# The weights' output rows parked in DRAM, lower halves of the weight sums on POOL, and a new issue list in an attention and FFN kernel

## The chip, the cores and the metric

One core of a Trainium2 chip. The metric is the device time of one execution in microseconds; for the kernel before it is 601.78 us, the median of 3 runs (601.61 to 604.16).

## The reference

```python
# q, k, v: (4, 8, 768, 64) fp32; blocks of 32 rows, a window of 16
k_sum = k.reshape(B, H, 24, 32, D).max(axis=3)
v_sum = v.reshape(B, H, 24, 32, D).mean(axis=3)
scores_l = where(|i - j| < 16, q @ k.T / 8, -1e9)      # local keys
scores_s = q @ k_sum.T / 8 + log(32)                    # 24 block maxima
a = softmax(concat[scores_l, scores_s])
x = (a @ concat[v, v_sum]) -> (3072 tokens, 512)
h = x @ w_in                        # 512 -> 2048
out = (s * relu(h)**2 + b) @ w_out  # 2048 -> 512
```

## The kernel before

The 3072 tokens are worked in 12 chunks c of 256 tokens, three to a batch entry. A chunk goes through attention by head pairs p (0 to 3), then through the FFN by 16 blocks f of 128 of the 2048 hidden columns; q is a pair of such blocks (0 to 7). Each fp32 matrix product is three TensorE products of upper and lower fp32r halves.

Every instruction is issued by `do(name)` from a list written out by hand, FIRST_ORDER and then REST_ORDER, under a manual schedule: the list's order is the order of every engine's and queue's instructions. Engines are in order, so an instruction that waits holds all behind it on its engine. The DMAs of this kernel all go through SP's queue (q1). Names in the list: a letter or two for the function, then numbers, chunk first.

- Attention of chunk c: u loads queries and keys (L253), k fills in the block maxima on POOL (L266), x and t load and fill the values (L260, L271), S scores on PE (L309), M masks on DVE (L332), E exponentials on ACT (L351), np and tb normalize and transpose on DVE (L365 to L368, L390), V values on PE (L441), X and y the upper and lower halves of the result (L227 on ACT, L457 on DVE). L loads the raw keys of a batch entry and K takes their block maxima (L154, L159); lv, vs, vm, sv do the same for the values' block means (L168, L175, L181, L186).
- FFN: H.f hidden block (L509, 24 matmuls to two blocks). For chunks 0 to 3, J, G, a, b square, scale and split it and P.f projects it (L554) into two "po" accumulators; O empties one of them on ACT (a copy at L227), z stores the rows (L701). For chunks 4 to 11, re, sq, af, sr, us, ls are the same steps (L567, L571, L575, L580 to L584, L591, L595), and p.q.n (L674) projects a pair of blocks by seven products of 128x256 blocks, n = 0 to 6, instead of eight. Its accumulators are called m, x, y, z: m lies in the "pav" bank, x and y in the two "po" banks, z in "pt". Three of the seven right-hand sides are sums of blocks of w_out, which are streamed from DRAM into a ring (j, L614), a fourth one is kept in the weights' own place (kc, L618).
- Weights: w, i, o load a block's w_in and w_out columns (L117), A and Bi, Bo, D turn them to fp32 tiles `w_f` (ACT L125 and L126, DVE L134 and L135), h makes the upper halves (L227), l the lower ones (DVE L147). `w_f` and `w_l` tiles share one pool of 16 buffers (wring). Once l has run, the fp32 tile is given up.
- Weight sums, while chunks 2 and 3 run: for each q, sw has six POOL steps, in which the first two (L629, 128x512) add upper and lower halves of the w_out part to get fp32 again and four more (L631 to L637, 128x256) make the sums. uw rounds to the upper half on ACT (L640, 128x1024), lw takes the lower half on DVE (L644, 128x1024), zw stores the two (L648, 512 KB each) to the DRAM tile `combos`. They work in `spare`, of three pieces of 1024 columns that are used in turn; `spare` and the ring of the later chunks are one buffer after the other in the same place, so the first j waits for the last zw.

The values' accumulator of head pairs 0 and 1 of chunk c is chosen in `values`: "po" where `c > SEVEN` (SEVEN is 4), else "pav", but for a few early chunks.

Of the kernel before, what the change touches and what calls it, by code (L numbers as in the profile page):

```python
# [14 lines left out]
ALU = mybir.AluOpType  # L15
# [21 lines left out]
UNIT = T + NSUB * KR + 2  # L37

# [6 lines left out]
def windowed_attention_then_relu2_ffn(ctx, tc, qk, vwin, kt, vt, kq, vrow, wp, out):  # L45
# [7 lines left out]
    ctx.enter_context(tc.tile_pool(name="gap_arena", bufs=1)).tile([P, 16], F32, name="gap_arena")  # L53
# [4 lines left out]
    ctx.enter_context(tc.tile_pool(name="gap_acts", bufs=1)).tile([P, 48], F32, name="gap_acts")  # L58
# [9 lines left out]
    spare = arena.tile([P, 3072], F32, name="spare", tag="ring")  # L68
    combos = kept.tile([NF // 2, P, 4, 2, 256], F32, name="combos")

# [65 lines left out]

    def upper_weights(f, other=False):
        j = f
        if j % 2 == 0:
            held["wh", j // 2] = slot(F32R, "wh")  # L140
        w_h[f] = held["wh", j // 2][:, 1024 * (j % 2) : 1024 * (j % 2 + 1)]
        copy(other, w_h[f], w_f[f])

    def lower_weights(f):

        w_l[f] = wring.tile([P, 1024], F32R, name="wl", tag="ring")
        nc.vector.tensor_tensor(w_l[f], w_f.pop(f), w_h[f].bitcast(F32), ALU.subtract)  # L147
# [271 lines left out]
    def values(c, p):  # L419
# [3 lines left out]
        elif c < 2 or p % 2 == 0:  # L423
            if c == 2:
                o_of[c, p] = ps_s.tile([P, 2 * T], F32, name="pav", tag="ps")
            elif c > SEVEN and p == 0:
                o_of[c, p] = ps_po.tile([P, 2 * T], F32, name="pav", tag="po")
            elif together(c) and p:
                o_of[c, p] = ps_t.tile([P, 2 * T], F32, name="pav", tag="pt")
            else:  # L430
                o_of[c, p] = ps_v.tile([P, 2 * T], F32, name="pav")
# [165 lines left out]
    def ring_part(c, q, n):  # L597
        if "ring" not in held:
            held["ring"] = arena.tile([P, 3072], F32R, name="ring", tag="ring")
# [8 lines left out]
        k = 512 * (3 * (q % 2) + n)  # L608
# [14 lines left out]

    def sums_of_weights(q, n):
        t = piece(2 * q)
        b11, b12, b21, b22 = (t[:, 256 * k : 256 * (k + 1)] for k in range(4))
        if n < 2:
            w = [x[2 * q + n][:, 512:].bitcast(F32) for x in (w_h, w_l)]
            nc.gpsimd.tensor_tensor(t[:, 512 * n : 512 * (n + 1)], *w, ALU.add)  # L629
        elif n == 2:  # L630
            nc.gpsimd.tensor_tensor(b22, b22, b12, ALU.add)  # L631
        elif n == 3:
            nc.gpsimd.tensor_tensor(b12, b12, b11, ALU.subtract)
        elif n == 4:
# [4 lines left out]
    def upper_weight_sums(q):  # L639
        nc.scalar.copy(piece(2 * q + 1).bitcast(F32R), piece(2 * q))  # L640

    def lower_weight_sums(q):
        t = piece(2 * q)
        nc.vector.tensor_tensor(t.bitcast(F32R), t, piece(2 * q + 1), ALU.subtract)  # L644

    def store_weight_sums(q, n):
        src = piece(2 * q + 1 - n)
# [55 lines left out]
    def evict(c, t, other=False):  # L703
# [4 lines left out]
    FIRST_ORDER = (  # L708
# [23 lines left out]
    )  # L732
    REST_ORDER = (
# [247 lines left out]
```

## Time and profile before

| | |
|---|---|
| median of 3 runs | 601.78 us (601.61 to 604.16) |
| the profiled execution | 602.11 us |
| its span | 600.4 us |
| busy: PE, DVE, ACT, POOL | 583.3, 438.6, 349.4, 298.8 us |
| DMA | 127.34 MB, mean 212 GB/s |
| mean granted TensorE clock | 0.994 |

The span is what the profiler saw between the first and the last instruction; the execution is 1.71 us longer. PE is busy 97% of the span. Times in the rows are counted from the span's start. In brackets stands the idle time of the engine ahead of an instruction and what released it.

### The profile page before, as it was taken

To read this page: it belongs to the slowest core of one execution; us is meant where nothing else is said; L and a number is where in the kernel's file an instruction comes from. 1 tells how busy PE (TensorE), PEld (TensorE's weight loads), DVE (VectorE), ACT (ScalarE), POOL (GpSimd) and SP (SyncE) were. 2 spreads that over 40 slices of the span, in tenths; PEclk is the share of its full clock that TensorE was granted. 3 is DMA by queue.
4 is the path that set the end of the run, shared out by engine and by line. 5 is a ranking of instruction groups with operands and counts; after the bars stand their busy time and mean duration, and the time that the engine had idled before them with its cause. 6 is when DMAs were issued, how large, how long until landed. Compare 5 with 4: busy or idle time off the path is not lost.

```text
span 600.4 us, 15345 instructions
## 1 busy us (share of the span) xinstructions
PE 583.3 (97%) x5816; PEld 554.0 (92%) x5816; DVE 438.6 (73%) x1033; ACT 349.4 (58%) x808; POOL 298.8 (50%) x499
## 2 busy tenths in 40 slices
PE   7999999999999999899999999999999999999996
PEld 6798898889799898799999999999999999999996
DVE  6999988799689699686688689588588488322323
ACT  5999999275496673733563564563563563433432
POOL 4330012591594563355655755745745745635643
PEclk9999999999999999799999999999999999999999
DMA  8999633064634974876776886766766766575540
GB/s 336 398 409 374 232 127 115 1 212 125 208 124 139 337 243 147 273 262 219 257 257 182 276 249 190 265 187 193 250 177 203 246 176 187 164 236 145 184 145 35
DMA packets 65401, 127.34 MB, mean 212 GB/s; under 512 B 7408, under 2 KB 17648, under 8 KB 65328
## 3 DMA queue, kind: packets, MB, share of 16 engines
q1 hardware_dynamic: 65328, 126.38, 63.4%
q8 instruction: 45, 0.74, 0.5%
q14 instruction: 28, 0.23, 0.1%
HBM read 111.52 MB, written 14.68 MB: 210 GB/s over the span
## 4 chain that ended last, share of the span: by engine, by line
PE 58%; DVE 16%; ACT 12%; DMA 8%; issue 3%; SPq 2%; POOL 1%; DVEq 0%; ACTq 0%; POOLq 0%
PE ph L509 28%; PE acc L674 24%; DVE pT L390 6%; PE pav L441 2%; DMA wraw<-in_wp_dram 2%; ACT wraw L125 2%; ACT wraw L126 2%; DMA ring<-combos 2%; DVE gs L541 2%; PE po L554 2%; ACT spare L351 2%; DVE spare L644 2%; PE ps L309 1%; DMA vraw<-in_vt_dram 1%; DMA combos<-spare 1%
## 5 line engine op out<-in xcount | busy, mean ns | idle before, releaser
L595 DVE TENSOR_TENSOR gs<-g,gs 128x896 fp32r<-128x896 f32 x64 | 71.1, 1112 | 97.6 <-ACT gs L591 97.1
L575 POOL TENSOR_SCALAR g<-g,sb_col 128x512 f32<-128x512 f32 x64 | 68.0, 1062 | 131.0 <-ACT g L571 118.2
L567 ACT ACTIVATE g<-ph 128x512 f32<-128x512 f32 x64 | 38.3, 598 | 158.5 <-PE ph L509 144.8
L390 DVE STREAM_TRANSPOSE pT<-qk 32x256 f32<-32x256 f32 x288 | 125.5, 436 | 4.8
L674 PE MATMUL acc<-wh,gs 128*128 128x256 f32 x512 | 121.2, 280 | 0.4 <-DVE gs L595 0.4
L509 PE MATMUL ph<-xh,wl 128*128 128x256 f32 x760 | 118.7, 278 | 0.2 <-DVE wl L147 0.2
L509 PE MATMUL ph<-xh,wh 128*128 128x256 f32 x760 | 117.3, 276 | 0.0
L509 PE MATMUL ph<-xl,wh 128*128 128x256 f32 x760 | 117.3, 276 | 0.0
L509 PEld LDWEIGHTS ph<-xh,wl 128*128 128x128 f32 x760 | 103.0, 188 | 4.1 <-DVE wl L147 1.0
L509 PEld LDWEIGHTS ph<-xl,wh 128*128 128x128 f32 x760 | 100.7, 188 | 0.0
L509 PEld LDWEIGHTS ph<-xh,wh 128*128 128x128 f32 x760 | 100.4, 188 | 0.0
L674 PE MATMUL acc<-ring,gs 128*128 128x256 f32 x558 | 96.4, 281 | 1.9 <-DMA ring<-combos 1.9
L674 PEld LDWEIGHTS acc<-wh,gs 128*128 128x128 f32 x512 | 91.3, 188 | 1.6 <-issue 0.9
L674 PEld LDWEIGHTS acc<-ring,gs 128*128 128x128 f32 x558 | 78.8, 188 | 2.6 <-DMA ring<-combos 2.5
L554 PE MATMUL po<-wh,gs 128*128 128x512 f32 x224 | 76.7, 394 | 0.1
L674 PE MATMUL acc<-wl,gs 128*128 128x256 f32 x256 | 71.3, 278 | 0.0
L591 ACT CAST gs<-g 128x896 fp32r<-128x896 f32 x64 | 59.9, 937 | 17.9 <-PE acc L674 7.1
L271 POOL COPY vw<-vsum 24x256 f32<-24x256 f32 x88 | 40.0, 490 | 45.2 <-DMA vw<-in_vwin_dram 18.1
L351 ACT ACTIVATE qk<-qk,mn 128x120 f32<-128x120 f32 x144 | 55.0, 384 | 6.5 <-DVE mn L332 5.7
L554 PE MATMUL po<-wl,gs 128*128 128x512 f32 x128 | 50.2, 392 | 0.0
L554 PEld LDWEIGHTS po<-wh,gs 128*128 128x128 f32 x224 | 42.1, 188 | 8.6 <-DVE gs L541 0.3
L580 POOL TENSOR_TENSOR g<-g 128x256 f32<-128x256 f32 x64 | 47.3, 738 | 4.7
(134 smaller groups left out, 919.2 us busy)
## 6 DMA issues: line engine op xcount, KB each, us to landing
ring<-combos SPq DMA_DIRECT2D x186, 256.0 KB
wraw<-in_wp_dram SPq DMA_DIRECT2D x32, 512.0 KB
qk<-in_qk_dram SPq DMA_DIRECT2D x44, 369.0 KB
vw<-in_vwin_dram SPq DMA_DIRECT2D x48, 256.0 KB
combos<-spare SPq DMA_DIRECT2D x16, 512.0 KB
out_dram<-o SPq DMA_DIRECT2D x24, 256.0 KB
kraw<-in_kt_dram SPq DMA_DIRECT2D x12, 384.0 KB
vraw<-in_vt_dram SPq DMA_DIRECT2D x12, 252.0 KB
```

What stands on the lines that cost most here:

```text
L125: nc.scalar.activation(top, top, AF.Prelu, scale=2.0**-112, alpha=2.0**32)
L271: nc.gpsimd.tensor_copy(vw_t[c, p][WIN:KR, e], vsum[bi][WIN : WIN + NB, 2 * p + e, :].unsqueeze(1).to_broadcast([NB, NSUB, D]),)
L351: nc.scalar.activation(pr, pr, AF.Exp, bias=mn_of[c, p][:, n : n + 1], scale=-1.0, accum_out=sums_of(c, p)[:, n : n + 1])
L390: nc.vector.transpose(to[BLOCK * k : BLOCK * (k + 1), :, rows], src)
L509: nc.tensor.matmul(ph, w[:, kc * P : (kc + 1) * P], x[:, kc], start=(n == 0), stop=(n == len(terms) - 1))
L554: nc.tensor.matmul(po[c, t], a[:, t * P : (t + 1) * P], w[:, 512:], start=(f == 0 and n == 0), stop=(f == NF - 1 and n == len(terms) - 1),)
L567: nc.scalar.activation(gg[c, q][:, : 2 * T], ph_of.pop((c, q)), AF.Relu)
L575: nc.gpsimd.tensor_scalar(g, g, s_col, b_col, ALU.mult, ALU.add)
L580: nc.gpsimd.tensor_tensor(g[:, 4:6], g[:, 0:1].to_broadcast([P, 2, P]), g[:, 1:3], ALU.subtract)
L591: nc.scalar.copy(halves[c, q][0], gg[c, q][:, P:])
L595: nc.vector.tensor_tensor(gl, gg.pop((c, q))[:, P:], gh.bitcast(F32), ALU.subtract)
L674: nc.tensor.matmul(to, g[:, k], w, start=(q == 0 and side == 0 and m == 0), stop=(q == NF // 2 - 1 and m == 2 and side == (bank != "m")),)
```

## The change

1. `park_weights` (pk0 to pk15) stores the fp32 tile's w_out part (128x512, 256 KB) to a DRAM tile `parked` after its conversion, and `w_f` is not given up by `lower_weights` any more. `load_parked` (lp0 to lp7) brings the parts of two blocks back (512 KB) into a piece of `spare`. The two POOL adds that had made fp32 out of the halves are gone, so sw has four steps.
2. The lower halves of the sums are two POOL subtracts of 128x512 (lw q.0 and q.1) instead of one DVE subtract of 128x1024.
3. The sums are worked in piece 0 or 1 by turns, and their upper halves always lie in piece 2.
4. Two unused gap tiles of 16 and 48 columns go; the arena is 3136 columns, of which the ring's parts begin at 16, so the ring's address stays.
5. In `values`, chunk 5's first accumulator is "pav" instead of "po".
6. One new list, ORDER. PE's instructions keep their order; SP, ACT, DVE and POOL get another one from chunk 2 on, and on SP the parks stand from u3.1 on.

The diff without the list:

```diff
+RING = 3136
...
-    ctx.enter_context(tc.tile_pool(name="gap_arena", bufs=1)).tile([P, 16], F32, name="gap_arena")
...
-    ctx.enter_context(tc.tile_pool(name="gap_acts", bufs=1)).tile([P, 48], F32, name="gap_acts")
...
-    spare = arena.tile([P, 3072], F32, name="spare", tag="ring")
+    spare = arena.tile([P, RING], F32, name="spare", tag="ring")[:, :3072]
     combos = kept.tile([NF // 2, P, 4, 2, 256], F32, name="combos")
+    parked = kept.tile([NF, P, 512], F32, name="parked")
...
+    def park_weights(f):
+        nc.sync.dma_start(parked[f], w_f[f][:, 512:])
...
-        nc.vector.tensor_tensor(w_l[f], w_f.pop(f), w_h[f].bitcast(F32), ALU.subtract)
+        nc.vector.tensor_tensor(w_l[f], w_f[f], w_h[f].bitcast(F32), ALU.subtract)
...
-            elif c > SEVEN and p == 0:
+            elif c > SEVEN + 1 and p == 0:
...
-            held["ring"] = arena.tile([P, 3072], F32R, name="ring", tag="ring")
+            held["ring"] = arena.tile([P, RING], F32R, name="ring", tag="ring")
...
-        k = 512 * (3 * (q % 2) + n)
+        k = 16 + 512 * (3 * (q % 2) + n)
...
+    def load_parked(q):
+        t = piece(q % 2).rearrange("p (f d) -> p f d", f=2)
+        nc.sync.dma_start(t, parked[2 * q : 2 * q + 2].rearrange("f p d -> p f d"))
+
     def sums_of_weights(q, n):
-        t = piece(2 * q)
-        b11, b12, b21, b22 = (t[:, 256 * k : 256 * (k + 1)] for k in range(4))
-        if n < 2:
-            w = [x[2 * q + n][:, 512:].bitcast(F32) for x in (w_h, w_l)]
-            nc.gpsimd.tensor_tensor(t[:, 512 * n : 512 * (n + 1)], *w, ALU.add)
+        b11, b12, b21, b22 = (piece(q % 2)[:, 256 * k : 256 * (k + 1)] for k in range(4))
+        if n == 0:
...
     def upper_weight_sums(q):
-        nc.scalar.copy(piece(2 * q + 1).bitcast(F32R), piece(2 * q))
-
-    def lower_weight_sums(q):
-        t = piece(2 * q)
-        nc.vector.tensor_tensor(t.bitcast(F32R), t, piece(2 * q + 1), ALU.subtract)
+        nc.scalar.copy(piece(2).bitcast(F32R), piece(q % 2))
+
+    def lower_weight_sums(q, n):
+        t, hi = (piece(k)[:, 512 * n : 512 * (n + 1)] for k in (q % 2, 2))
+        nc.gpsimd.tensor_tensor(t.bitcast(F32R), t, hi, ALU.subtract)
...
-        src = piece(2 * q + 1 - n)
+        src = piece((2, q % 2)[n])
...
-    FIRST_ORDER = (
...
-    REST_ORDER = (
+    ORDER = (
...
-        for name in (FIRST_ORDER + " " + REST_ORDER).split():
+        for name in ORDER.split():
```

SP's queue from the last unit of chunk 3 on, before (`wraw` are weight tiles, `kraw` raw keys, `qk` units, `out_dram` the first rows of the result):

```order
L253 DMA qk<-in_qk_dram 128x738
L154 DMA kraw<-in_kt_dram 128x768
L117 DMA wraw<-in_wp_dram 128x1024 x4
L253 DMA qk<-in_qk_dram 128x738 x2
L117 DMA wraw<-in_wp_dram 128x1024 x6
L154 DMA kraw<-in_kt_dram 128x768
L260 DMA vw<-in_vwin_dram 128x512
L701 DMA out_dram<-o 128x512 x2
```

and after (`parked` are the new stores; line numbers are 3 higher):

```order
L256 DMA qk<-in_qk_dram 128x738
L138 DMA parked<-wf 128x512 x9
L157 DMA kraw<-in_kt_dram 128x768
L117 DMA wraw<-in_wp_dram 128x1024 x4
L256 DMA qk<-in_qk_dram 128x738 x2
L138 DMA parked<-wf 128x512
L117 DMA wraw<-in_wp_dram 128x1024 x2
L138 DMA parked<-wf 128x512 x2
L117 DMA wraw<-in_wp_dram 128x1024 x2
L138 DMA parked<-wf 128x512 x2
L117 DMA wraw<-in_wp_dram 128x1024 x2
L157 DMA kraw<-in_kt_dram 128x768
```

Nine stores now stand ahead of the raw keys and of the weight tiles that follow, and five more between the later weight tiles.

ACT at the start of chunk 4's FFN, before (L567 and L571 are re and sq, L591 us, L640 the cast of the weight sums, L181 a mean of values, L227 with `o<-po` O3.0):

```order
L571 ACTIVATE g<-g 128x512
L640 CAST spare<-spare 128x1024
L567 ACTIVATE g<-ph 128x512
L591 CAST gs<-g 128x896
L571 ACTIVATE g<-g 128x512
L181 ACTIVATE vmean<-vhalf 96x64
L567 ACTIVATE g<-ph 128x512
L591 CAST gs<-g 128x896
L227 COPY o<-po 128x512
L571 ACTIVATE g<-g 128x512
L567 ACTIVATE g<-ph 128x512
L227 CAST xh<-pav 128x512
```

and after:

```order
L570 ACTIVATE g<-ph 128x512
L574 ACTIVATE g<-g 128x512
L570 ACTIVATE g<-ph 128x512
L574 ACTIVATE g<-g 128x512
L594 CAST gs<-g 128x896
L230 COPY o<-po 128x512 x2
L570 ACTIVATE g<-ph 128x512
L594 CAST gs<-g 128x896
L574 ACTIVATE g<-g 128x512
L570 ACTIVATE g<-ph 128x512
L230 CAST xh<-pav 128x512
```

The cast and the mean have left this place, and the two copies out of "po" stand right behind the first us.

SP's queue ahead of the ring's first loads, before (L648 are the stores of the weight sums, L253 units of chunk 6, L186 and L168 the values' block means, L614 the ring):

```order
L648 DMA combos<-spare 512x1x256
L253 DMA qk<-in_qk_dram 128x738
L648 DMA combos<-spare 512x1x256
L253 DMA qk<-in_qk_dram 128x738 x3
L186 DMA vsum<-vmean 24x64 x4
L168 DMA vraw<-in_vt_dram 96x672
L701 DMA out_dram<-o 128x512
L614 DMA ring<-combos 128x512 x6
```

and after:

```order
L651 DMA combos<-spare 512x1x256
L621 DMA wh<-combos 128x256
L256 DMA qk<-in_qk_dram 128x738 x2
L621 DMA wh<-combos 128x256
L621 DMA wl<-combos 128x256
L651 DMA combos<-spare 512x1x256
L621 DMA wh<-combos 128x256
L621 DMA wl<-combos 128x256
L617 DMA ring<-combos 128x512 x6
L256 DMA qk<-in_qk_dram 128x738 x2
```

The ring's loads now stand two kept sums behind the last store, and ahead of the last two units and of the means.

## Rows read from the trace of the kernel before

**Rows 1.** The page's first line.
```profile
span 600.4 us, 15345 instructions
```

**Rows 2.** PE's waits: engine, line, what it waited for: us in total, times, longest.
```profile
PE pav L441 <- issue: 2.9, 1, 2.9
PE acc L674 <- DMA ring<-combos: 1.9, 2, 1.2
PE ps L309 <- POOL qk L266: 1.0, 2, 0.6
```

**Rows 3.** Timeline of PE, 238 to 262: start us, us, engine line op out<-in xcount [idle before].
```profile
238.48 0.62 PE L509 MATMUL ph<-xh,wh 128*128 128x256 f32 x4
242.01 3.68 PE L441 MATMUL pav<-pT,vw 120*64 120x64 f32 x64 [2.91 <-issue]
...
260.00 0.62 PE L674 MATMUL acc<-ring,gs 128*128 128x256 f32 x3 [1.23 <-DMA ring<-combos]
...
261.88 0.62 PE L509 MATMUL ph<-xh,wl 128*128 128x256 f32 x4
```

**Rows 4.** Windows: stretch, us; busy of PE, PEld, DVE, ACT, POOL; PEclk, DMA, GB/s.
```profile
243.00:246.00 3.00, 3.00 (x59) 2.88 (x60) 0.69 (x1) 1.63 (x4) 2.81 (x8) 0.50 0.66 174
```

**Rows 5.** The chain of waits, one chunk later: start us, us, engine, out, line, count.
```profile
293.35 2.02 PE pav L441 x64
...
297.17 5.15 PE acc L674 x42
...
307.49 2.73 PE ph L509 x24
```

**Rows 6.** Timeline of ACT, 240 to 242.
```profile
240.00 0.60 ACT L567 ACTIVATE g<-ph 128x512 f32<-128x512 f32 x1 [6.98 <-DVE gs L595]
...
241.32 0.59 ACT L227 COPY o<-po 128x512 f32<-128x512 f32 x1
```

**Rows 7.** Timeline of DVE, 232 to 240.
```profile
232.13 5.87 DVE L390 STREAM_TRANSPOSE pT<-qk 32x256 f32<-32x256 f32 x13
...
238.83 1.08 DVE L595 TENSOR_TENSOR gs<-g,gs 128x896 fp32r<-128x896 f32 x1
```

**Rows 8.** Timeline of PE, 158 to 164.
```profile
158.19 2.08 PE L441 MATMUL pav<-pT,vw 120*64 120x64 f32 x64
...
163.46 0.50 PE L554 MATMUL po<-wh,gs 128*128 128x512 f32 x1
```

**Rows 9.** Groups by line and shape: count, busy us, mean ns, idle before.
```profile
L629 POOL TENSOR_TENSOR spare<-wh,wl 128x512 f32<-128x512 f32 x16 | 23.4, 1478 | 3.2 <-DMA combos<-spare 1.6 <-DVE spare L644 1.4
L644 DVE TENSOR_TENSOR spare<-spare 128x1024 fp32r<-128x1024 f32 x8 | 10.6, 1327 | 2.8 <-ACT spare L640 2.7
L175 DVE TENSOR_REDUCE vhalf<-vraw 96x21 f32<-96x672 f32 x12 | 10.0, 843 | 0.4 <-DMA vraw<-in_vt_dram 0.4
```

**Rows 10.** Windows at loads, at stores, and at both.
```profile
54.00:57.00 3.00, 3.00 (x25) 2.84 (x24) 2.83 (x5) 3.00 (x6) 0.00 (x0) 1.00 1.02 414
57.00:60.00 3.00, 3.00 (x15) 2.38 (x13) 2.48 (x4) 3.00 (x6) 0.00 (x0) 1.00 0.56 213
126.00:129.00 3.00, 3.00 (x24) 2.84 (x23) 2.96 (x19) 2.54 (x12) 2.88 (x5) 1.00 0.98 299
186.50:187.00 0.50, 0.50 (x6) 0.50 (x6) 0.49 (x2) 0.50 (x2) 0.42 (x2) 1.00 0.96 373
187.00:187.50 0.50, 0.50 (x7) 0.50 (x6) 0.49 (x2) 0.50 (x1) 0.50 (x1) 1.00 0.39 148
```

**Rows 11.** Timelines of SP, ACT, DVE and PE, 64 to 83.
```profile
64.04 0.33 SPq L154 DMA_DIRECT2D kraw<-in_kt_dram  x1
...
73.50 1.14 ACT L125 ACTIVATE wraw<-wraw 128x1024 f32<-128x1024 f32 x1 [0.89 <-DMA wraw<-in_wp_dram]
...
81.34 1.21 DVE L147 TENSOR_TENSOR wl<-wf,wh 128x1024 fp32r<-128x1024 f32 x1
...
82.70 0.71 PE L509 MATMUL ph<-xh,wl 128*128 128x256 f32 x4
```

More of the change, by code (lines that the diff above doesn't have):

```diff
@@ L622, in piece @@
         return spare[:, 1024 * n : 1024 * (n + 1)]
+    def load_parked(q):
+        t = piece(q % 2).rearrange("p (f d) -> p f d", f=2)
+        nc.sync.dma_start(t, parked[2 * q : 2 * q + 2].rearrange("f p d -> p f d"))
     def sums_of_weights(q, n):
-        t = piece(2 * q)
-        b11, b12, b21, b22 = (t[:, 256 * k : 256 * (k + 1)] for k in range(4))
-        if n < 2:
-            w = [x[2 * q + n][:, 512:].bitcast(F32) for x in (w_h, w_l)]
-            nc.gpsimd.tensor_tensor(t[:, 512 * n : 512 * (n + 1)], *w, ALU.add)
+        b11, b12, b21, b22 = (piece(q % 2)[:, 256 * k : 256 * (k + 1)] for k in range(4))
+        if n == 0:
+            nc.gpsimd.tensor_tensor(b22, b22, b12, ALU.add)
+        elif n == 1:
+            nc.gpsimd.tensor_tensor(b12, b12, b11, ALU.subtract)
         elif n == 2:
[L631 to L634, printed above, removed]
             nc.gpsimd.tensor_tensor(b11, b11, b22, ALU.subtract)
@@ L705, in evict @@
         copy(other, out_of[c, t], po[c, t])
-    FIRST_ORDER = (
[23 rows of a table removed]
-    )
-    REST_ORDER = (
[159 rows of a table removed]
+    ORDER = (
[181 rows of a table added]
     )
@@ L907, in windowed_attention_then_relu2_ffn @@
         "Y": hidden_part, "H": hidden, "J": activate, "G": scaled, "a": upper_rows, "b": lower_rows,
-        "P": project, "O": evict, "z": store_rows, "h": upper_weights, "l": lower_weights,
-        "af": affine, "cr": clear_rim, "cb": combine, "kc": keep_combo, "j": load_combo, "lv": load_v,
-        "ls": lower_sums, "lw": lower_weight_sums, "np": normalize_pair, "p": project_seven, "re": rectified,
-        "sv": spread_v, "sq": squares, "zw": store_weight_sums, "sr": sums_of_rows, "sw": sums_of_weights,
-        "tb": turned_blocks, "us": upper_sums, "uw": upper_weight_sums, "vm": v_mean, "vs": v_sum,
+        "P": project, "O": evict, "z": store_rows, "h": upper_weights, "l": lower_weights, "pk": park_weights,
+        "af": affine, "cr": clear_rim, "cb": combine, "kc": keep_combo, "j": load_combo, "lp": load_parked,
+        "lv": load_v, "ls": lower_sums, "lw": lower_weight_sums, "np": normalize_pair, "p": project_seven,
+        "re": rectified, "sv": spread_v, "sq": squares, "zw": store_weight_sums, "sr": sums_of_rows,
+        "sw": sums_of_weights, "tb": turned_blocks, "us": upper_sums, "uw": upper_weight_sums, "vm": v_mean,
+        "vs": v_sum,
     }
```

363 rows, old and new, of tables (FIRST_ORDER, ORDER, REST_ORDER) are left out of this document.

## The prediction

> **What bounds the kernel now.** The page comes first: the span is 600.4 us [rows 1], and its list of busy times puts TensorE (PE) at 97% of it. So only what lets PE stand idle, runs it at the lower clock, or takes matmuls away can move the time. The diff takes none away, and PE's instructions stand in the same order, so I read PE's waits [rows 2]. Those that come after the first weights are few: 2.9 us at the values of an attention chunk (L441), 1.9 us at the streamed ring (L674), 1.0 us at scores (L309). The timeline of PE places the first two in one stretch [rows 3]. The last matmul of H4.7 starts at 238.48 and takes 0.62; V5 starts only at 242.01, after 2.91 us of nothing. What follows is slower too: V5 takes 3.68 us [rows 3], where the same step of the next chunk takes 2.02 in the chain of waits [rows 5]. The granted clock says why: it is 0.50, the 1.2 GHz level, between 243 and 246 [rows 4], right behind the idle stretch. Then come two waits for the ring, the one with its row 1.23 us long [rows 3].
>
> So the stretch is measured whole. Unstalled, V5 could start when H4.7's last matmul lets go; 24 such matmuls take 2.73 us [rows 5], so the last four are through in 0.45 and V5 is due at 238.93. H4.10 starts at 261.88 [rows 3]: 22.95 us later. The same list of products one chunk later runs from 293.35 to 307.49 [rows 5]: 14.14 us. The excess is **8.81 us**, of which only 2.91 is the idle time itself.
>
> The second place is one chunk earlier: V3 starts at 158.19 and P2.8 at 163.46 [rows 8], 5.27 us, against 293.35 to 297.17 = 3.82 [rows 5] for the same V and S work. The excess is **1.45 us**.
>
> **Why V5 waits.** Before, the accumulator of V5.0 is one of the two "po" banks, so it needs O3.0 to have emptied it. O3.0 is ACT's copy at 241.32, 0.59 long [rows 6], and ends 0.1 before V5. ACT is in order: ahead of it stands re4.2 (L567, 240.00), which sat 6.98 us for ls4.0 on DVE (L595). ls4.0 runs at 238.83, behind 5.87 us of transposes of chunk 5 and a block sum of 0.88 [rows 7]. So DVE's backlog reaches PE by way of ACT's order.
>
> **The change part by part.**
>
> *Order and accumulator.* O3.0 and O3.1 move ahead of re4.2 on ACT, and V5.0 goes to the "pav" bank, which chunk 4's values left long ago. Either alone cuts the chain. What is late next: V5 itself needs chunk 5's transposes, which ended at 232.13 + 5.87 = 238.00 even before [rows 7], 0.9 us ahead of 238.93; p4.0.0 needs ls4.0 and, newly, y5.0 out of "pav". In the new order ls4.0 and ls4.1 stand directly behind the transposes. X5.0 on ACT stands behind re4.3; with H4.7's last matmul ending at 239.1, re4.3 (0.60 [rows 6]) ends at 239.7; X5.0, a copy of the size of O3.0's 0.59, at 240.3; y5.0, narrower than ls4.0's 1.08 [rows 7], by 241.4. p4.0.0 is due at 238.93 + 3.82 = 242.75. Slack 1.3 us.
>
> *DVE's load ahead of V5.* Three lower halves (lw5 to lw7) of 1327 ns and three block sums of 843 ns [rows 9] leave DVE there: 3 × 1.33 + 3 × 0.84 = 6.5 us. K2.0 and K2.1, which each wait for a transfer, come before chunk 5's normalization instead. So the transposes end about 231.5, or at worst where they do now.
>
> *The ring.* Its first six loads were issued behind the last store of sums and other transfers; now that store is issued at about P3.11 and the loads at H4.2, ahead of the second pair of chunk 6's units and of z3.0. The two waits go. These edits take the whole of it: **−8.81**, taken whole since each rung of the chain is cut and the next reader has slack. Bounds: nothing goes (0), or all.
>
> *S4.* P2.8's stall is two waits for POOL's fills [rows 8], which wait for chunk 4's units, whose buffers are freed by chunk 3's transposes. Those transposes now stand grouped ahead of the block sums, and the loads of u4.0 to u4.3 stand earlier: **−1.45**, between −1.45 and 0.
>
> *POOL.* Sixteen adds of 128x512 at 1478 ns go [rows 9], sixteen subtracts of the same shape come: no change there. DVE loses eight operations of 1327 ns, 10.6 us [rows 9], hidden under PE except as told above. ACT's eight casts stay. Cost 0; if POOL were late, uw would stand in ACT's queue with the a and G of chunks 2 and 3 behind it (a rival below).
>
> *Parking.* Sixteen stores of 256 KB and eight loads of 512 KB join SP's queue. The loads (4.2 MB in 110 us) lie where no wait of PE names a transfer. The stores matter early: nine of them (2.36 MB) now stand ahead of L1.0 and of w15 and w10. Before, the DMA engines are full to 57 and 0.56 busy from 57 to 60 [rows 10], so they come free at 57 + 0.56 × 3 = 58.7, and L1.0 is issued at 64.04 [rows 11]. No store of this size from SBUF runs there in the trace, so it is bounded: an output store of 256 KB alone moves 373 and then 148 GB/s in two half microseconds [rows 10], (373 + 148) × 0.5 = 260 KB, so 373 while it runs; the busiest later stretch with stores in it gives 299 [rows 10]. At 373 the nine take 2.36 MB / 373 = 6.3 us and end at 65.0, 1 us behind the old issue of L1.0; at 299, 7.9 us and 66.6. What hangs on it: ACT waits 0.89 for a weight tile at 73.50; DVE runs the lower weights of block 10 at 81.34, and PE's reader starts at 82.70 right behind [rows 11]. No slack there. A delay of the whole end of the stores past 64.04 would be 1.0 at 373 and 2.6 at 299. I take **+0.4**, from 0 to +2.6: nearer to the 373 row, since that is a plain store like these, and under its 1.0, since the loads behind can still share the engines with the last stores.
>
> A word of the Trainium skill weighs in here ("DMA: Bandwidth & Descriptors", section "Bandwidth"): it puts HBM-to-SBUF transfers at about 358 GB/s for a core. The trace differs: 414 GB/s in the loads from 54 to 57 [rows 10], so the measurement decides. By the page the nine stores would take an estimated 6.6 us, and the sum would be 0.3 us higher.
>
> A wf buffer is now free only when its store has landed too; l7 is the first tile that takes over such a buffer, of block 0, whose store is the first of the nine. It lies inside the same +0.4.
>
> **Sum.** The profiled execution took 602.11, its span 600.4: 602.11 − 8.81 − 1.45 + 0.4 = 592.25. The median of the three runs is 601.78, 0.33 lower, so **592.0** for the median (591.9, rounded up).
>
> **The rivals.** (1) *Part of the V5 stretch stays*: DVE's transposes wait behind K2.0 and K2.1 by more than the 6.5 us gained, or y5.0 outlasts its 1.3 us of slack, so that p4.0 or V5 waits 1 to 3 us and the clock falls again. For it: after 2.91 us of idle the clock fell [rows 4]; DVE is the busy engine there. Against: the transposes had 0.9 us of slack even at the old load. About half of the 8.81 stays: 592.0 + 4.4 = 596.4, from 594 to 598.
>
> (2) *The S4 stall stays or turns up elsewhere*, since the sums' chain (POOL add, ACT cast, POOL subtract, two stores) now shares one upper piece and POOL does both ends: 592.0 + 1.45 = 593.5. This is also "the change does not do what it says", for the earlier units.
>
> (3) *The parks cost more*, near the 299 row or with weights 12 to 14 late behind stores that stand between their loads: 592.0 + 1.5 to 2.5 = 593.5 to 594.5.
>
> (4) *Slower than before*: the stores run far below 373 and hold the weight loads behind them in the queue. The place is L1.0, w15 and w10 at 64.04. The gain of 10.26 is used up when nine stores take 16.6 us instead of 6.3, at 2.36 MB / 16.6 = 142 GB/s; the second half microsecond of the output store shows 148 [rows 10], but that is its tail. At 120 GB/s it would be 19.7 us, 3.1 past that point: 604.9. For it: a DRAM write of these is seen nowhere under full loads. Against: the 299 row has loads and stores of small rows mixed.
>
> **How the numbers follow.** Chances: my forecast 0.52 (590.5 to 593.3), rival 2 0.14, rival 3 0.12, rival 1 0.16, rival 4 0.06. The range runs from 590.5 (parks free, and a little more of the clock back) to 598.0, the top of rival 1; outside it I leave rival 4, the worst of rival 1 and a gain beyond what I count: some 0.15. The measurement can tell 0.5%, 3 us, from no change: faster means under 598.8. Faster then holds the forecast, rivals 2 and 3 and most of rival 1: 0.86. Same (598.8 to 604.8): the rest of rival 1 and half of rival 4, with parks and S4 falling together: 0.09. Slower: 0.05.
>
> **What would show it.** In the profile of the changed kernel: among PE's waits no entry at L441, none at the ring and none at the scores of chunk 4; V5 to H4.10 in about 14.1 us and V3 to P2.8 in about 3.8; the granted clock at 1.00 in all that stretch; the activation of A10, the lower weights of block 10 and PE's reader within 0.5 us of 73.50, 81.34 and 82.70; POOL's new subtracts near 1.48 us each. Wrong would be: a gap at p4.0.0 on y5.0, transposes of chunk 5 ending later than 238.0, or weight tiles more than 2 us late before 110 us.

## The result, and the profile after

The changed kernel takes 593.92 us (median of 4 runs, 593.17 to 594.16) against 602.31 for the kernel before in the same runs: a ratio of 0.985, with a 95% interval of 0.983 to 0.987. The forecast was 592.0 with a range of 590.5 to 598.0. The time lies in the range, 1.9 us above the forecast. It is outside the band that the forecast itself was given (590.5 to 593.3) and inside the one of rival 3, the parks that cost more (593.5 to 594.5). Of the gain, 601.78 − 592.0 = 9.8 us had been forecast and 8.4 came.

The first line of the page of the changed kernel, then the start of its list of PE's waits (engine, line, what it waited for: us in total, times, longest):

```profile
span 592.2 us, 15380 instructions
```

```profile
PE ps L315 <- DMA kq<-in_kq_dram: 4.2, 1, 4.2
PE ph L512 <- ACT r L520: 1.0, 1, 1.0
PE pt L404 <- ACT pT L230: 0.7, 2, 0.4
PE po L557 <- DVE gs L544: 0.5, 1, 0.5
```

The three waits of [rows 2] are gone. The 4.2 us at the first scores were there before (4.3). New is 1.0 us at the hidden block (L512) for ACT.

The chain of waits of the changed kernel gives the places of the forecast's steps (start us, us, engine, out, line, count):

```profile
119.05 2.02 PE pav L444 x64
...
160.38 2.02 PE pav L444 x64
...
164.20 2.96 PE po L557 x12
...
239.76 2.02 PE pav L444 x64
241.78 1.80 PE ps L312 x64
243.58 5.15 PE acc L677 x42
...
253.90 2.73 PE ph L512 x24
```

V3 to P2.8 is 164.20 − 160.38 = 3.82 us, where [rows 8] had 5.27. V5 to H4.10 is 253.90 − 239.76 = 14.14, where [rows 3] had 22.95 from V5's due time on. Both are the sizes that were worked out. Chunk 4's units, whose fills the scores behind V3 had waited for, on SP before and after:

```profile
155.01 1.79 SPq L253 DMA_DIRECT2D qk<-in_qk_dram  x4
```

```profile
142.11 1.25 SPq L256 DMA_DIRECT2D qk<-in_qk_dram  x2
```

The windows show the clock at full, where [rows 4] had 0.50:

```profile
242.00:245.00 3.00, 3.00 (x76) 2.84 (x68) 2.41 (x17) 2.22 (x10) 2.81 (x7) 1.00 0.94 283
245.00:248.00 3.00, 3.00 (x28) 3.00 (x27) 2.40 (x19) 1.65 (x6) 0.09 (x1) 1.00 1.00 327
```

What is missing from the gain lies ahead of all that. V2 starts at 119.05, where the same row of the kernel before is 2.13 us earlier:

```profile
116.92 2.02 PE pav L441 x64
```

From V2 to the end it is 592.2 − 119.05 = 473.15 us now and was 600.4 − 116.92 = 483.48: a gain of 10.33, against 8.81 + 1.45 = 10.26 forecast. So between the two profiled executions (602.11 and 593.89 us, forecast 592.25) the whole difference to the forecast is one term, the parks: 2.13 us, where the sum had 0.4. The timeline of ACT shows the weight tiles that came late (in brackets the idle time and what ended it). The rows are the first conversions of blocks 15, 10 and 14, called A15, A10 and A14 below; the second answers to the 73.50 of [rows 11]:

```profile
71.61 1.18 ACT L125 ACTIVATE wraw<-wraw 128x1024 f32<-128x1024 f32 x1 [1.52 <-DMA wraw<-in_wp_dram]
...
75.06 1.16 ACT L125 ACTIVATE wraw<-wraw 128x1024 f32<-128x1024 f32 x1 [1.22 <-DMA wraw<-in_wp_dram]
...
99.18 1.14 ACT L125 ACTIVATE wraw<-wraw 128x1024 f32<-128x1024 f32 x1 [0.47 <-DMA wraw<-in_wp_dram]
```

A10 is 1.56 us late, and PE waits 1.0 for the activation behind it. A14, at 99.18, is 2.11 late, another 0.55; in the kernel before it is

```profile
97.07 1.16 ACT L125 ACTIVATE wraw<-wraw 128x1024 f32<-128x1024 f32 x1
```

So in this profile a sign of being right that the prediction named fails, since A10, and with it the lower weights of block 10 (82.90 for 81.34), is not within 0.5 us of its old place; and a sign of being wrong is there, a weight tile more than 2 us late.

### The profile page after: what moved, and what is told of

It reads as the page before. It is cut to its first block, busy times and chain, and to the rows that moved or that the text cites. A ratio compares the mean times of both kernels' runs of the same rounds, so it can differ in the third digit from the quotient of the medians.

```text
span 592.2 us, 15380 instructions
## 1 busy us (share of the span) xinstructions
PE 579.7 (98%) x5816; PEld 551.2 (93%) x5816; DVE 429.7 (73%) x1025; ACT 352.3 (59%) x808; POOL 313.6 (53%) x499
## 4 chain that ended last, share of the span: by engine, by line
PE 80%; DMA 9%; DVE 5%; ACT 3%; issue 1%; POOL 1%; SPq 0%; DVEq 0%; POOLq 0%; ACTq 0%
PE ph L512 38%; PE acc L677 25%; PE po L557 10%; DMA wraw<-in_wp_dram 6%; PE pav L444 3%; PE ps L312 3%; DMA parked<-wf 1%; ACT pr L354 1%; DVE wf L135 1%; DMA kq<-in_kq_dram 1%; DVE spare L335 1%; DVE wf L134 1%; POOL g L583 0%; ACT wraw L125 0%; DVE wl L150 0%
## 5 line engine op out<-in xcount | busy, mean ns | idle before, releaser
L512 PE MATMUL ph<-xh,wl 128*128 128x256 f32 x760 | 118.9, 278 | 1.2 <-ACT r L520 1.0
L512 PE MATMUL ph<-xh,wh 128*128 128x256 f32 x760 | 117.4, 276 | 0.0
L512 PE MATMUL ph<-xl,wh 128*128 128x256 f32 x760 | 117.4, 276 | 0.0
L578 POOL TENSOR_SCALAR g<-g,sb_col 128x512 f32<-128x512 f32 x64 | 54.8, 856 | 114.0 <-ACT g L574 105.7
L512 PEld LDWEIGHTS ph<-xh,wl 128*128 128x128 f32 x760 | 103.0, 188 | 5.4 <-ACT r L520 1.2
L512 PEld LDWEIGHTS ph<-xl,wh 128*128 128x128 f32 x760 | 100.7, 188 | 0.0
L512 PEld LDWEIGHTS ph<-xh,wh 128*128 128x128 f32 x760 | 100.5, 188 | 0.0
L583 POOL TENSOR_TENSOR g<-g 128x256 f32<-128x256 f32 x64 | 72.0, 1125 | 4.8
L274 POOL COPY vw<-vsum 24x256 f32<-24x256 f32 x88 | 44.0, 536 | 20.4 <-DMA vw<-in_vwin_dram 10.6
```

The costliest lines, as they stand in the source:

```text
L274: nc.gpsimd.tensor_copy(vw_t[c, p][WIN:KR, e], vsum[bi][WIN : WIN + NB, 2 * p + e, :].unsqueeze(1).to_broadcast([NB, NSUB, D]),)
L512: nc.tensor.matmul(ph, w[:, kc * P : (kc + 1) * P], x[:, kc], start=(n == 0), stop=(n == len(terms) - 1))
L578: nc.gpsimd.tensor_scalar(g, g, s_col, b_col, ALU.mult, ALU.add)
L583: nc.gpsimd.tensor_tensor(g[:, 4:6], g[:, 0:1].to_broadcast([P, 2, P]), g[:, 1:3], ALU.subtract)
```

## Experiments on the early loss

**The changed kernel again, and without its stores.** For a run, a few differences are of use: V2's start, the time from V2 to the end, which the early part can't touch, and within the early part the distance from the tile ahead (the start of the last L125 on half a tile ahead of A15) to A10, and from A10 to A14. The two other kernels leave out the first nine (the lines shown) or all sixteen pk names of the list, and their loads have another source, so that they don't compute the reference's result:

```diff
-        nc.sync.dma_start(t, parked[2 * q : 2 * q + 2].rearrange("f p d -> p f d"))
+        nc.sync.dma_start(t, vwin[q, 0:2].rearrange("f p e i d -> p f (e i d)"))
...
-pk0 pk1 pk2 pk3 pk4 pk5 pk6 pk7 pk8
```

> The changed kernel once more, beside the others of this call. Both theories: 593.5 to 594.5 us, A10 on ACT at about 75.06 and V2 on PE at about 119.05. If these two lie more than 0.5 us elsewhere, the early loss varies from run to run and is not the parks' alone.

> The sixteen stores to the parked tile are left out, and the eight loads read as many bytes of the values' input instead, so the weight sums and the last eight chunks' results are not the reference's. Theory (the stores take the early 2.13 us): A10 on ACT back from 75.06 to 73.5, V2 on PE back from 119.05 to 116.9, the time 2.1 us under the changed kernel, about 591.8. Rival (the new order of the list takes them): V2 stays at about 119, the time at 593.9.

> Only the first nine stores (ahead of the raw keys' and two weight tiles' loads) are left out; loads read the values' input, so the sums are not the reference's. Theory (two places: 1.56 us at A10 by the nine, 0.5 at A14 by later ones): A10 at 73.5, V2 at about 117.4, time about 592.3. Rival (the nine do all of it): V2 at 116.9. Rival (it is the later ones): V2 at 119.

Measured: 593.83 us for the changed kernel (median of 4, 593.30 to 594.25), 592.04 without any store, 593.66 without the first nine (one run each). Without any store V2 starts at 117.10, with the new list as it is; so the stores take the early time, and the rival, the list's order, is out. Without the first nine V2 is at 118.74, nearer to the rival (119, the later stores) than to the theory (117.4). And the changed kernel itself has A10 and V2 (117.85) 1.4 and 1.2 us earlier in its second profile than in its first: by the sign set down for it, the early loss varies from run to run.

The windows show that the stores do fill the gap that the prediction saw; the stretch is 58 to 64, first with all stores, then without any (columns as in [rows 4]):

```profile
58.00:64.00 6.00, 6.00 (x66) 5.16 (x65) 5.56 (x8) 5.94 (x10) 0.00 (x0) 1.00 1.05 402
```

```profile
58.00:64.00 6.00, 6.00 (x66) 5.17 (x65) 5.58 (x8) 5.94 (x11) 0.00 (x0) 1.00 0.11 41
```

But A10 does not follow them cleanly. With all the stores, the second profile of the very same kernel has

```profile
70.24 1.18 ACT L125 ACTIVATE wraw<-wraw 128x1024 f32<-128x1024 f32 x1 [0.22 <-DMA wraw<-in_wp_dram]
73.66 1.14 ACT L125 ACTIVATE wraw<-wraw 128x1024 f32<-128x1024 f32 x1 [1.21 <-DMA wraw<-in_wp_dram]
```

and without the first nine it is

```profile
71.02 1.21 ACT L125 ACTIVATE wraw<-wraw 128x1024 f32<-128x1024 f32 x1 [0.29 <-DMA wraw<-in_wp_dram]
74.62 1.13 ACT L125 ACTIVATE wraw<-wraw 128x1024 f32<-128x1024 f32 x1 [1.36 <-DMA wraw<-in_wp_dram]
```

Part of the latter is an offset of 0.7 us that this run has from 35 us on, long before the stores. Taken from the tile ahead, over all the profiles that have the tile loads in this order:

| us | with the stores in question | without them |
|---|---|---|
| tile ahead of A15 to A10 (first nine) | 7.67, 6.26, 6.90, 6.69 | 6.02 (before), 6.49, 6.53, 6.44, 6.14, 6.08, 5.99 |
| A10 to A14 (the later ones) | 24.12, 24.40, 24.17, 24.18, 24.22, 24.34 | 23.57 (before), 23.60, 23.70, 23.95, 23.59, 23.59, 23.56 |
| V2 starts at (all) | 119.05, 117.85, 118.67, 118.03 | 116.92 (before), 117.10, 117.26, 117.23, 117.60, 117.46, 116.61 |
| V2 to the end (first nine) | 473.15, 473.05, 473.13, 473.37 | 473.2, 472.96, 473.36 |

(Runs that are told below are in it. With stores, the first two values are the two profiles of the changed kernel, the third and fourth the changed kernel with two edits undone and with the lower halves back on DVE; the last two of the second row are the kernel without the first nine and one that keeps six of the later stores. Without stores, the last two values of the first row and the last four of the next two come from the old list; two of its runs are not in the first row, because A10 waits for DVE there. The last row has the new list alone, without the run with adds, of which more below.) So stores cost V2 1.2 us in the mean (118.40 against 117.17), and there the two columns don't overlap. The later stores cost 0.6 of it, and that is steady: again the columns don't overlap. The nine early ones cost between nothing and 1.6 us, 0.6 in the mean of these few; this distance varies by 0.5 even without them, and the columns overlap, so that the nine cost anything is likely and not shown. The first size, 1.56, was one draw. V2 to the end is 473.0 to 473.4 whatever stands early.

**Stores later.** Six stores stay ahead of the raw keys, three go behind the two tiles; two units and a later store move too:

```diff
-pk6 pk7 pk8 L1.0 w15 w10 u3.2 u3.3 pk9 w12
+L1.0 w15 w10 pk6 pk7 pk8 pk9 w12 u3.2 u3.3
...
-pk13 x2.2
+x2.2 pk13
```

> Six stores stay ahead of the raw keys; three move behind the two weight tiles, two chunk-3 units move behind the weight tiles of block 12, and one later store moves behind a values' load. Everything is computed. Theory (bytes queued ahead of the tiles are what costs): A10 at 73.5 to 74.2, V2 at 117 to 118, time 592 to 593. Rival (stores cost wherever they stand, since they share the engines with the same loads): V2 at 119, time 593.9.

Measured: 594.71 us (593.44 to 595.25, 4 runs), with A10 at 74.81 and V2 at 118.49. Not better, and the theory's times are missed: from the tile ahead to A10 it is 7.64 with six stores ahead, as long as the longest with nine. Moving a third of the bytes back bought nothing that shows over the spread.

**Adds instead of parking.** All stores and loads of parked rows go, the fp32 tile is given up once l has run, and the two POOL adds come back at the first sum:

```diff
-        nc.sync.dma_start(t, parked[2 * q : 2 * q + 2].rearrange("f p d -> p f d"))
+        for n in range(2):
+            w = [x[2 * q + n][:, 512:].bitcast(F32) for x in (w_h, w_l)]
+            nc.gpsimd.tensor_tensor(t[:, n], *w, ALU.add)
```

> The changed kernel's list, but without parking: the two POOL adds per pair of blocks are back (directly ahead of the first sum), the stores and loads of the parked tile are gone. Everything is computed. Theory (the parks are pure cost early on, and POOL has room for 23.4 us more): V2 on PE at about 117.0, V2 to the end 473.1 as in the changed kernel, 592.0 us. Rival (the adds make POOL late, ACT waits at its cast of the sums and PE behind that): V2 to the end 475 to 480, 594 us or more.

Measured: 593.61 us (592.53 to 595.21, 5 runs; ratio to the kernel before 0.9846, 0.982 to 0.987). V2 starts at 117.26, near the 117.0 of the theory, and the stretch from V2 to V5 is as long as in the changed kernel to 0.15 us, so POOL does have the room. But V2 to the end is 591.9 − 117.26 = 474.64, 1.5 more than the theory had, and the time misses its 592.0. In the profiled run one wait for the ring, far from the sums, took most of the early gain back:

```profile
298.45 0.62 PE L679 MATMUL acc<-ring,gs 128*128 128x256 f32 x3 [1.11 <-DMA ring<-combos]
```

This row stands in a chunk where nothing of the weight sums is left to do, and no other profile of the new list has it. Whether adds bring it about wasn't settled. In time the two ways are the same.

**Parking for the last six blocks alone.** The names pk0 to pk9 go, and for q up to 4 the two adds of the run above, directly ahead of the first sum, take the place of the load:

```diff
+        if q > 4:
+            nc.sync.dma_start(t, parked[2 * q : 2 * q + 2].rearrange("f p d -> p f d"))
+        else:
+            for n in range(2):
+                w = [x[2 * q + n][:, 512:].bitcast(F32) for x in (w_h, w_l)]
+                nc.gpsimd.tensor_tensor(t[:, n], *w, ALU.add)
```

> The changed kernel with parking for the last six blocks alone; the first ten get their fp32 back by two POOL adds per pair, as before, so the nine early stores and one more are gone, and one later store stands behind a values' load. Everything is computed. Theory (early stores cost 0.2 to 1.6 us at the two weight tiles, later ones 0.3): V2 at 117.0 to 117.6, V2 to the end 473.1, 591.7 to 592.5 us. Rival (what differs between runs is the chip's own, not the stores): V2 anywhere from 117 to 119, the median within 0.5 us of 593.8.

Measured: 592.81 us (592.41 to 593.46, 4 runs), V2 at 117.44 and 473.36 to the end, as the theory said; the time is 0.3 above its range. It is the lowest median of the kernels that compute everything, 1.0 under the changed kernel's 593.83, but its ratio to the kernel before, 0.9838 (0.981 to 0.986), can't be told from the changed kernel's 0.9839 (0.981 to 0.987). The A10-to-A14 cost is still there (24.34).

## Experiments on the V5 stretch

Each kernel of this section was run once; what is read from it is the trace, and the times go beside medians of 602.8 to 603.2 us of the kernel before.

The prediction put the stall down to O3.0, held in ACT's queue behind re4.2, and said of two edits, the copies ahead of re4.2 and the pav bank, that either alone cuts the chain.

**Both undone in the changed kernel.**

```diff
-            elif c > SEVEN + 1 and p == 0:
+            elif c > SEVEN and p == 0:
...
-us4.0 ls4.0 O3.0 O3.1 z3.0 z3.1 re4.2 us4.1
+us4.0 ls4.0 re4.2 us4.1 O3.0 O3.1 z3.0 z3.1
```

> The changed kernel with both of these undone: chunk 5's first accumulator is in po again, and the two copies stand behind re4.2 and its us on ACT. Theory (DVE's earlier transposes alone also cut the chain, since re4.2 no longer waits for ls4.0): V5 waits under 0.3 us, V5 to H4.10 14.1 to 14.5, V2 to the end 473.1 to 473.6. Rival (the copies' place is what counts): V5 waits 1 to 3 us, the clock falls, V2 to the end 476 to 479.

Measured: 593.55 us, no wait at V5, V2 to the end 591.8 − 118.67 = 473.13, as the theory said. Nothing is lost. The two edits aren't needed once DVE is early: in the changed kernel the transposes and ls4.0 stand in the timeline of DVE as

```profile
225.42 6.76 DVE L393 STREAM_TRANSPOSE pT<-qk 32x256 f32<-32x256 f32 x15
233.71 1.09 DVE L598 TENSOR_TENSOR gs<-g,gs 128x896 fp32r<-128x896 f32 x1 [1.53 <-ACT gs L594]
```

against 232.13 and 238.83 in [rows 7], though the early loss, less the gain at S4, has shifted V5's due time by 0.7 us (238.93 to 239.60).

**Both done in the kernel before, and nothing else; then with the ring's loads (the last two lines) earlier too.** The line of the copies stands for where they are now:

```diff
-            elif c > SEVEN and p == 0:
+            elif c > SEVEN + 1 and p == 0:
...
+O3.0 O3.1 re4.2 us4.1
...
-sv2.0 lv2.1.2 z3.0 j4.0.0 j4.0.1 j4.0.2 j4.1.0 j4.1.1 j4.1.2
+j4.0.0 j4.0.1 j4.0.2 j4.1.0 j4.1.1 j4.1.2 sv2.0 lv2.1.2 z3.0
```

> The kernel before with two edits alone: the two copies out of po ahead of re4.2 on ACT, and chunk 5's first accumulator in the pav bank. Theory (both the copy's place and the ring's late loads make up the 8.81 us): V5 starts without a wait, 0.1 to 0.3 us behind H4.7, but p4.0 then waits for the ring, whose loads stay where they were: V5 to H4.10 18 to 20 us, time 597 to 599. Rival (the copy's place is all of it, the ring waits were only its echo): 14.1 to 14.5 us, time 593.5. Rival (DVE's backlog holds V5 or p4 anyway): 21 to 23 us, time 601.

> As the run with the two edits, and the ring's first six loads are issued ahead of the values' means, a values' block and the stored rows on SP. Theory: the ring waits go or fall under 1.5 us; V5 to H4.10 14.2 to 16.5 us, time 594 to 596, with what is left at p4.0 on y5.0 (ls4.0 is still late at 238.8). Rival (DVE's backlog): 18 us or more.

Measured: 606.08 and 610.88 us, both slower than before, and no theory had that. V5 starts without a wait, but S6 behind it does not, and from V5's due time to H4.10 it is 27.0 and 31.3 us (22.95 before). Of the first run, ACT, DVE and PE:

```profile
241.28 0.59 ACT L227 COPY o<-po 128x512 f32<-128x512 f32 x1 [8.37 <-PE pav L441]
247.89 0.59 ACT L227 COPY o<-po 128x512 f32<-128x512 f32 x1 [6.02 <-DMA out_dram<-o]
248.37 0.60 ACT L567 ACTIVATE g<-ph 128x512 f32<-128x512 f32 x1
...
251.02 0.60 ACT L567 ACTIVATE g<-ph 128x512 f32<-128x512 f32 x1 [0.69 <-DVE gs L595]
```

```profile
239.36 1.08 DVE L595 TENSOR_TENSOR gs<-g,gs 128x896 fp32r<-128x896 f32 x1
240.36 0.84 DVE L175 TENSOR_REDUCE vhalf<-vraw 96x21 f32<-96x672 f32 x1
```

```profile
238.92 2.08 PE L441 MATMUL pav<-pT,vw 120*64 120x64 f32 x64
249.07 0.66 PE L309 MATMUL ps<-qk 64*64 64x120 f32 x4 [8.07 <-issue]
251.67 3.46 PE L309 MATMUL ps<-qk 64*64 64x120 f32 x60 [1.93 <-ACT g L567]
```

O3.0 sat for 8.37 us. The profile names PE, but its accumulator was finished at 233.5. What ends just ahead of 241.28 is the sum of raw values on DVE, 240.36 + 0.84 = 241.20; in the second run it is the same, 240.94 and 241.02. The copy's output tile comes from a staging pool of two buffers that raw keys, raw values and output rows share, and it takes over one that this sum still reads. O3.1 then waits 6.02 for the first rows' store, which stands on SP behind the values' means. With the copies first on ACT, all of re4.2 and what follows stands behind both, and S6's scores take the banks that re4.2 and re4.3 empty (they end at 248.97 and 251.62, and S6's two parts start at 249.07 and 251.67). In the second run the store is later by the ring's loads, and O3.1 waits 11.02.

So with the two edits the wait leaves V5 and turns up, longer, at S6: the copies have a second wait, for the output buffer, which the prediction did not see. In the kernel before it did not show, because there O3.0 stands behind re4.2 and is later than the sum anyway. In the changed kernel the loads and sums of these values stand behind the copies, which run without a wait at 233.65. Either of the two edits by itself, the bank above all, was not run in the old list.

**The sums of values moved alone, and the lower halves alone, in the kernel before.**

```diff
-tb5.0.3.3 sr4.1.1 H4.5 vs2.1.0 vm2.0 u6.0 sr4.1.2 u6.1 sv2.0 ls4.0 H4.6 lv2.1.2 vs2.1.1 re4.2
+tb5.0.3.3 sr4.1.1 H4.5 u6.0 sr4.1.2 u6.1 ls4.0 H4.6 re4.2
...
+z3.1 lv2.0.0 lv2.0.1
...
+p4.1.6 vs2.0.0
```

```diff
-        nc.vector.tensor_tensor(t.bitcast(F32R), t, piece(2 * q + 1), ALU.subtract)
+        u = piece(2 * q + 1)
+        for n in range(2):
+            h = slice(512 * n, 512 * (n + 1))
+            nc.gpsimd.tensor_tensor(t[:, h].bitcast(F32R), t[:, h], u[:, h], ALU.subtract)
```

> The kernel before, with the last batch entry's block sums of the values (loads, sums on DVE, means, spreading, and chunk 6's fills that read them) behind chunk 6's masks, as in the changed kernel, and nothing else. Theory (O3.0 is held by these sums, first through DVE's queue and then because its output tile takes over a buffer that they still read): V5 waits under 0.5 us behind H4.7, V5 to H4.10 14.1 to 16 us, time 594 to 596. Rival (the lower halves on DVE and the order of the copies matter as much): V5 still waits 1 to 3 us, V5 to H4.10 18 us or more, time 598 to 602.

> The kernel before with the lower halves of the weight sums on POOL (two subtracts of 128x512 for one of 128x1024 on DVE), the list as it was. Theory (DVE's backlog falls by 3 x 1.33 us ahead of V5, and the sums of the values with it): V5's wait falls from 2.91 to 0 to 1 us, V5 to H4.10 15 to 19 us, V3 to P2.8 4.5 to 5.3, time 595 to 599. Rival (POOL, which still has the adds, brings the sums late): a wait for the ring over 2 us, or ACT waiting at its casts, time 601 or more.

Measured: 609.89 us for the first, 599.42 for the second. Both theories are missed. With the sums moved, ACT's copy no longer waits for a buffer (240.38, directly behind re4.2's rows). But the transposes are no earlier (231.97 for 232.13): the raw keys are loaded 0.8 to 1.2 us later on SP, and from their block maxima on DVE is busy without a gap. V5 waits 1.15, and the loads of values now stand ahead of the ring's on SP; from V5's due time to H4.10 it is 24.6 us. DVE's ls4.0, PE and SP:

```profile
237.88 1.09 DVE L595 TENSOR_TENSOR gs<-g,gs 128x896 fp32r<-128x896 f32 x1
```

```profile
241.07 2.09 PE L441 MATMUL pav<-pT,vw 120*64 120x64 f32 x64 [1.15 <-issue]
...
247.53 0.62 PE L674 MATMUL acc<-ring,gs 128*128 128x256 f32 x3 [1.67 <-DMA ring<-combos]
260.22 1.01 PE L674 MATMUL acc<-ring,gs 128*128 128x256 f32 x3 [4.77 <-DMA ring<-combos]
```

```profile
250.81 5.53 SPq L168 DMA_DIRECT2D vraw<-in_vt_dram  x2
256.43 2.75 SPq L614 DMA_DIRECT2D ring<-combos  x6
```

With the lower halves on POOL, ls4.0 is 2.6 us earlier (236.25 for 238.83), V5 still waits 1.51 and the ring 1.91 and 1.59. DVE's ls4.0, then PE:

```profile
236.25 1.08 DVE L595 TENSOR_TENSOR gs<-g,gs 128x896 fp32r<-128x896 f32 x1
```

```profile
239.43 2.08 PE L441 MATMUL pav<-pT,vw 120*64 120x64 f32 x64 [1.51 <-issue]
241.44 1.87 PE L309 MATMUL ps<-qk 64*64 64x120 f32 x64
246.14 0.91 PE L677 MATMUL acc<-ring,gs 128*128 128x256 f32 x3 [1.91 <-DMA ring<-combos]
```

From V5's due time to H4.10 this run takes 21.30 us (22.95 before), and V3 to P2.8 4.22 (5.27 before): a fifth of the one gain and most of the other.

The two runs and the kernel before time the prediction's chain to V5. From the end of ls4.0 to the start of V5 it is 239.91 to 242.01, 238.97 to 241.07 and 237.33 to 239.43: 2.10 us each time, with re4.2, us4.1 and O3.0 on ACT in between. So in the old list V5 does hang on ls4.0, as the prediction has it. In the changed kernel ls4.0 ends at 234.80, 4.8 us ahead of V5's due time (239.60), and the chain has more than its 2.10 us.

**The lower halves back on DVE in the changed kernel.**

```diff
-        t, hi = (piece(k)[:, 512 * n : 512 * (n + 1)] for k in (q % 2, 2))
-        nc.gpsimd.tensor_tensor(t.bitcast(F32R), t, hi, ALU.subtract)
+        t, hi = piece(q % 2), piece(2)
+        if n == 0:
+            nc.vector.tensor_tensor(t.bitcast(F32R), t, hi, ALU.subtract)
```

> The changed kernel with the lower halves of the weight sums back on DVE, one subtract of 128x1024 each, where the first of the two POOL subtracts stood. Theory (with the block sums out of the way DVE has room for 10.6 us more, so the move to POOL is not needed): V2 to the end 473.1 to 473.6 us, V3 to P2.8 3.82, V5 to H4.10 14.14. Rival (the move to POOL carries part of the gain): a stall at V3's or V5's scores comes back, V2 to the end 474.5 to 478.

Measured: 594.02 us, V2 to the end 473.37, no stall at V3 or V5, as the theory said. The move to POOL isn't needed in the new list, as little as the copies' place. No run takes back the move, the copies' place and the bank together, so that the list alone would do isn't shown.

## Why the prediction was right, point by point

- **The excess of the V5 stretch, 8.81 us**: the stretch now takes the 14.14 us that it was to take, so all of 22.95 − 14.14 = 8.81 is gone. Sizing a stall by the same list of products one chunk later, and not by its 2.91 us of idle time, took in the low clock and the ring's waits.
- **S4, 1.45 us**: measured 5.27 − 3.82 = 1.45. Two of chunk 4's units are now issued at 142.11, where all four stood at 155.01. The run with the lower halves alone on POOL, which has the old list, already has most of it, so DVE's load was part of that cause.
- **That the next reader has slack**: p4.0.0 was to be due 1.3 us behind y5.0. In the second profile of the changed kernel y5.0 runs from 240.32 for 0.69, and p4.0.0 starts at 242.31, 1.30 later.
- **POOL at no cost**: its sixteen subtracts took 1412 ns each, against 1478 for the adds of [rows 9], and PE waits for POOL nowhere behind V2.
- **The parks, +0.4**: the term of the sum that was too small. In the first profile they cost 2.13; over all profiles V2 is 1.2 us later with stores; from the medians it is 10.33 less the 8.39 to 9.35 that the two comparisons gained, 1.0 to 1.9. The end of the nine stores at 65.0 was about right: at the 402 GB/s of the window above, 2.36 MB take 5.9 us and end at 64.6. What the nine cost, 0.6 in the mean, is near the 0.4, but not clear of the spread, so it doesn't bear out the working. What the sum left at nothing are the later stores, between weight tiles: they cost 0.6, and the prediction has them in rival 3 alone. The bound of 2.6 held both, and the time came out at rival 3's. That it lies in the range is no luck, but the forecast's own band was missed by this term, and by a kernel before that ran 0.5 us slower than its 601.78.
- **Why the stall goes**: the chain of the prediction, ls4.0, re4.2, O3.0, V5, is what holds V5 in the old list (2.10 us from the end of ls4.0 to V5 in three profiles), and the new list frees it at its root, by ls4.0 5.1 us earlier. The step "either alone cuts the chain" was not enough of an argument: with both, V5 starts on time and the wait moves to S6, by the shared staging buffers. Taking back the copies' place and the bank together, or the move to POOL, loses nothing in the new list; in the old list the groups that were tried change V2 to the end by −2.4 us (the move to POOL), +3.7 (copies and bank), +6.8 (the sums) and +8.1 (copies, bank and ring). The total was right because the list removes DVE's lateness, the buffers' wait and the ring's late place together, and the forecast took the stretch as a whole. Which smallest set of moves is enough wasn't found.
- **The chances**: 0.86 for "faster" is too low for its own parts. Rival 1 was put at 594 to 598, wholly under 598.8, so with the forecast and rivals 2 and 3 it makes 0.94. Rival 2 is out: its 593.5 is near the time, but V3 to P2.8 is 3.82.

## What to carry to other kernels

Size a stall by the distance between the same two steps where nothing stalls, and then ask of each edit whether it removes a wait or only the last name on it: an instruction moved ahead in an in-order queue takes its other waits with it, and an output tile from a small shared pool is one of them. Transfers put into a gap of the DMA engines are not the only ones to count: here the stores left between later loads cost as much (0.6 us) as the nine in the gap, and the sum had them at nothing. One profile is too little to size such a loss; the same kernel gave 2.13 and 0.93. To find a loss of 1 us in runs that differ by 1 us, cut the trace at a step behind which all runs agree (here V2 to the end, within 0.4 but for the one run with a ring wait of its own) and compare the two sides apart.

## What the runs showed of the hardware

From 30 to 57 us the loads run at 400 to 424 GB/s (windows of 3 us, kernel before), and the stores right behind them at 402, above the 373 of [rows 10]. The Trainium skill ("DMA: Bandwidth & Descriptors", section "Bandwidth") gives about 358 for each core when both cores of a memory domain stream, and 425 measured for a core alone. The trace agrees with the second, and the 358 that the prediction took from there was not the one for this case. How soon a given tile lands behind them differs between profiles of one kernel by more than 1 us (A15 at 71.61 and 70.24), which was unexpected next to the later stretch. POOL's add of 128x256 in the activation (64 of them) took 738 ns in the mean before and 1125 after, and its multiply 1062 and 856, with the same instructions. This goes with the kernel and not with the run: the add takes 736 to 739 in every profile of the old list and 1096 to 1125 in every one of the new. PE doesn't wait for POOL behind V2, and the cause wasn't looked for.
